# Third batch's combining weights finished among the experts, conversions paused while the first sums are copied, last store split: a fused linear-attention, soft-MoE and feed-forward kernel

## The chip, the core and the metric

The kernel runs on one core of a Trainium2 chip. The metric is device time in microseconds (us) of one execution, taken as the median of several runs. Five engines work side by side, each on its own queue in program order: TensorE (PE, matrix products, with its weight loads shown as PEld), VectorE (DVE), ScalarE (ACT), GpSimd (POOL) and SyncE (SP), which here issues all DMAs. They meet at semaphores: an instruction that has to wait holds everything behind it on its engine. PE writes to PSUM, which has eight banks of 128 x 512 floats; DVE and ACT read them out.

## The reference, cut to what matters

Three stages follow each other. `attn` is a gated linear recurrence over 768 steps for 4 batches of 8 heads of 48; its output is laid out as 3072 tokens of 384. `moe` is a soft mixture of 8 experts with 4 slots each, and `moe2` a feed-forward layer with 2048 hidden units.

```python
for t in range(S):                                   # attn
    cur = einsum('bhd,bhe->bhde', u * kt, vt)
    y[:, :, t] = einsum('bhd,bhde->bhe', rt, state + cur)
    state = wt[:, :, :, None] * state + einsum('bhd,bhe->bhde', kt, vt)
...
logits = x @ phi                                     # moe: x is 3072 x 384, phi 384 x 32
d = softmax of logits over the tokens                # dispatch: each slot's mix of tokens
slot_input = d.T @ x
slot_out[e] = relu(slot_input[e] @ w1[e]) @ w2[e]    # 8 experts
c = softmax of logits over the 32 slots              # combining weights of each token
x = c @ slot_out
...
h = x @ w_in                                         # moe2
out = (h * sigmoid(1.702 * h)) @ w_out
```

All is float32. w_in and w_out come as 8-byte floats and are turned into float32 on the chip.

## The kernel before

`phase_a` computes the recurrence in chunks and, per batch of 768 tokens, the logits. `phase_b` runs the experts on the 32 slot inputs. `phase_c` is the dense stage. There c @ slot_out is never formed as 384 columns: slot_out @ w_in is a table of 32 x 2048 (`mst`, two halves of 1024 columns), and each token needs only its 32 combining weights. The transposed combining weights of all tokens lie in `cT`; a matrix product with 128 columns of `mst` gives the hidden values of 512 tokens. To keep float32 accuracy, the operands are split into a high part (fp32r, a rounded copy) and a low part (the rest), and the terms are added by more products or, for `cT` and `mst`, by four 32-row blocks in one product.

**Combining weights of a batch** (`Batch.combining`, a generator in two parts, then `combined`): the first part subtracts each token's maximum and takes exponentials (L890 to L892). The second (L895 to L906) sums, divides, and writes high and low parts to two `c4` tiles: eight DVE instructions and two POOL copies. `combined` (L914) transposes three 128 x 128 blocks of a `c4` tile into a PSUM bank on PE, and ACT copies the bank to its home in `cT`. Batches 0 and 1 are done in `phase_a`. For batches 2 and 3 (`comb`), `phase_b` runs the first part.

**The dense stage's units.** The main loop of `phase_c` has 96 units n, each a pair (block tb of 512 tokens, block f of 128 hidden values). For units 0 to 15 the blocks f = 0 to 7 of token blocks 0 and 1 alternate; units 16 to 47 take token blocks 2 to 5 one after the other, f = 0 to 7; units 48 to 95 are f = 8 to 15 of all six. A unit is: `act` (one product into a `pa` bank, L1089; two such banks), `gelu` (ACT, L1096), `high` (ACT cast to `gh`, L1103), `low` (DVE subtraction to `gl`, L1111), and `project` (nine products of 128 x 512 into three `po` banks, L1127: `gh` with w_out's high part, `gh` with its low part, `gl` with the high part). Up to unit 15 the order is by term, later by bank. Each of `g`, `gh`, `gl` has three buffers. In unit n the order of issue is high(n+1), act(n+3), gelu(n+2), low(n+1), the specials of that unit, project(n).

After its first eight f, a token block's sums are copied from the three `po` banks to memory (`keep`, L1141: two copies on DVE, one on ACT), in units 14, 15, 23, 31, 39 and 47. After the last eight, `store` adds bank and kept sum on DVE (L1147) and stores the 128 x 512 result (L1148); three such stores per token block.

**Conversions.** In nearly every unit of the first half some step of an 8-byte-to-4-byte conversion follows project: three DVE instructions (L290, L291, L293), one on ACT (L298), two on DVE (L302, L303), and for w_out a split into high and low (ACT L194, DVE L196). Which starts when stands in `begin`; one step of each running conversion is issued per unit (`going`). Pieces of w_in's second half (`late`, three steps) start in units 12, 14, ..., 26.

**Batches 2 and 3 in the loop.** The second part of `combining` was issued in unit 17 for batch 2 and unit 25 for batch 3, and the six transposes (into `po` banks of the token block that is not in work) with two ACT copies in units 20 and 28, before project.

**The dense stage's preparation** (from the first `scaled` to the loop): folding the expert outputs, the table's first half, `keep_warm` (dummy products into a bank that nobody reads, so that PE works while it waits, L280), four `act`, two `gelu`/`high`/`low`, `project(0)`, `gelu(2)`. Its PSUM banks: `pt` and `prs[0]`, `prs[1]` for the table, and two `pa` banks, the first of which (`pm`) held the table.

Of the kernel before, what the change touches and what calls it, by code (L numbers as in the profile page):

```python
# [14 lines left out]
ALU = mybir.AluOpType  # L15
# [256 lines left out]
def run(steps):  # L272
    for _ in steps:
        pass


def keep_warm(nc, room, idle, n):

    for _ in range(n):
        nc.tensor.matmul(room, idle[:, 512:640], idle[:, 0:512], start=True, stop=True)  # L280
# [647 lines left out]
def phase_b(tc, W, after, late, sp, sT, soft, batches=(), ebias=None):  # L928
    nc = tc.nc
    con, ident, phis, cT, SI, negm, Zs = soft  # L930
    psA = after.enter_context(tc.tile_pool(name="psA", reuse_waits="tile", bufs=2, space=PSUM))
    mid = ExitStack()
    psH = mid.enter_context(tc.tile_pool(name="psH", bufs=1, space=PSUM, reuse_waits="tile"))
    psS = mid.enter_context(tc.tile_pool(name="psS", bufs=2, space=PSUM, reuse_waits="tile"))
    with late:
        bp = late.enter_context(tc.tile_pool(name="bp", bufs=1, reuse_waits="tile"))
        own = ExitStack()
        w2q = own.enter_context(tc.tile_pool(name="w2q", bufs=1, side="right", reuse_waits="tile"))
        W.load2(4 if batches else 3, pool=w2q)
        sTm = bp.tile([128, KT, NE * 36], F32, name="sTm")  # L940
        nc.gpsimd.memset(sTm, 0.0)
        hTm = bp.tile([128, HT, NE * 36], F32, name="hTm")
        h = W.slot(W.place_out[3])
        flat = hTm.rearrange("p f s -> p (f s)")
        step = W.in_steps(ebias, {0: flat, 1: flat[:, 1024:], 4: h[:, 512:]}) if batches else lambda *a: None

        def own_slots(t):

            return t.rearrange("p k (e q) -> p k e q", q=36)[:, :, :, 0:SPE]

        fold = con[:, OFF_SEL:OFF_SEL + NS]
        nc.vector.tensor_copy(own_slots(sTm), sT.rearrange("p k (e s) -> p k e s", s=SPE))

        pz = psS.tile([128, 512], F32, name="ps")
        nc.tensor.matmul(pz[:, 0:1], con[:, OFF_SEL:OFF_SEL + 128], Zs[:, B - 1:B], start=True, stop=True)
        scale = Zs[:, 0:1]
        nc.vector.tensor_scalar_add(scale, pz[:, 0:1], 1e-9)
        nc.vector.reciprocal(scale, scale)


        def room():
            return sp.tile([128, 12 * NS], F32, name="c4", bufs=3)

        comb = [bt.combining(room) for bt in batches[2:]]
        for it in comb:
            next(it)
        nc.scalar.activation(bp.tile([128, 1], F32, name="tiny"), con[:, 0:1], AF.Gelu_apprx_sigmoid)
        step(0, 0)
        step(0, 1)
        step(1, 0)  # L970
        step(1, 1)
        step(0, 2)
        ph = psH.tile([128, 512], F32, name="ps")
        for n, p in enumerate((3, 0, 1, 2)):
            for kt in range(KT):
                for j in range(4):
                    e = p + 4 * (j % 2)
                    nc.tensor.matmul(ph[32 * j:32 * j + 32], sTm[:, kt, 36 * e - 4 * p:36 * e - 4 * p + 32],  # L978
                                     W.a[e][j // 2][:, kt], start=(n == 0 and kt == 0), stop=(n == 3 and kt == KT - 1))
            if n == 0:  # L980
                step(1, 2)
                step(2, 0)
                step(2, 1)
                nc.scalar.copy(hTm, con[:, OFF_MASK:OFF_MASK + 1].unsqueeze(2).to_broadcast([128, HT, NE * 36]))
            if n == 1:
                step(2, 2)
                step(3, 0)
                if batches:
                    cT.room(1, F32R)
            W.turn(n)  # L990
        for q in range(2):
            nc.scalar.activation(h[:, 256 * q:256 * q + 256], ph[:, 256 * q:256 * q + 256], AF.Relu)
        step(3, 1)
        h4 = h[:, 0:512].rearrange("p (q c r) -> p q r c", q=2, r=2)
        for q in range(2):
            pt = psS.tile([128, 2, 128], F32, name="ps")
            for r in range(2):
                nc.tensor.transpose(pt[:, r], h4[:, q, r], ident)
            for r in range(2):
                nc.vector.tensor_copy(own_slots(hTm)[:, 2 * q + r::4].rearrange("p f (g e) s -> p f g e s", g=2),  # L1000
                                      pt[:, r].rearrange("p (f g e s) -> p f g e s", f=2, g=2, s=SPE)[:, :, :, 0:4])
        po = psH.tile([128, 512], F32, name="ps")
        for e in range(NE):
            for i0 in range(0, HT, 4):
                for j in range(4):
                    nc.tensor.matmul(po[32 * j:32 * j + 32, 0:DM], hTm[:, i0 + j, 32 * e:32 * e + 32],  # L1006
                                     W.b[e][:, i0 + j], start=(e == 0 and i0 == 0), stop=(e == NE - 1 and i0 > 0))
            if e == 0:
                rep = W.slot(W.place_c[0], F32R)
                nc.gpsimd.memset(rep[:, 0:1024].bitcast(F32), 0.0)  # L1010
                rep4 = rep[:, 0:1024].rearrange("p (q n a s) -> p q n a s", q=2, n=4, a=4)
                for i in range(2):
                    nc.gpsimd.tensor_copy(rep4[:, i, :, i::2],
                                          ident.rearrange("p (n s) -> p n s", n=4).unsqueeze(2).to_broadcast([128, 4, 2, NS]))
            for m, i in (((3, 2), (4, 0), (4, 1)), ((5, 0), (5, 1), (4, 2)), ((5, 2),))[e] if e < 3 else ():
                step(m, i)
            if e == 4:
                own.close()
                cvp = after.enter_context(tc.tile_pool(name="cvp", bufs=1, side="right", reuse_waits="tile"))
    return comb, cvp, room, psA, mid, psH, psS, po, rep  # L1020


def phase_c(tc, W, after, dense, ebias, soft, out, check=None, batches=()):
# [3 lines left out]
    with ExitStack() as c2:  # L1027
# [115 lines left out]
        def store(tb):  # L1143

            for i in range(KT):
                os_ = gp.tile([128, 512], F32, name="os", bufs=3)
                nc.vector.tensor_tensor(out=os_, in0=live["po", tb][i], in1=sums[tb][:, i], op=ALU.add)  # L1147
                nc.sync.dma_start(out=out[i * 128:(i + 1) * 128, tb * 512:tb * 512 + 512], in_=os_)  # L1148

        def open_psO():  # L1150
            nonlocal psO
# [4 lines left out]
        def bank(a, i):  # L1156
            return psO.tile([128, 512], F32, name=f"po{a}{i}")
# [23 lines left out]
        step(1, 0)  # L1181
        act(0)
        act(1)
        keep_warm(nc, pt, idle, 7)
        gelu(0)
        place(0, 1, prs[1], nc.vector.tensor_copy)
        high(0)
# [11 lines left out]
        act(3)  # L1199
        project(0)  # L1200
        gelu(2)
        step(2, 2)
        step(3, 0)

# [11 lines left out]
        for n in range(1, n_all):  # L1216
            high(n + 1)
            act(n + 3)
            gelu(n + 2)
            low(n + 1)  # L1220
            if n == t1 + 1:
                pm = bank(0, 0)
                table(1, pm)
            if n == t1 + 2:
                table_high(1, pm)
                table_low(1, pm)
            if n == t1 + 3:
                prs = [bank(0, 1 + q) for q in range(2)]
                for q in range(2):
                    repeat(1, q, prs[q])  # L1230
            if check and n == n_all - FH + 2:
                check.result(room(), bank(0, 0))
            for k, (bt, it) in enumerate(zip(batches[2:], comb)):
                if n == FH * (k + 2) + 1:
                    run(it)
                if n == FH * (k + 2) + 4:
                    for i in range(2):
                        nc.scalar.copy(bt.home(i), bt.combined(i, bank(1 - k, i)))
            project(n)
            if n == t1 + 3:  # L1240
                place(1, 0, prs[0], nc.scalar.copy)
                place(1, 1, prs[1], nc.vector.tensor_copy)
            if order[n][1] == FH - 1:
                keep(order[n][0])
            if order[n][1] == FT - 1:
                store(order[n][0])
            if n in begin:
                f, m, k = begin[n]
                going.append([f, m, 0, k])
            for q in going:  # L1250
                q[0](q[1], q[2])
                q[2] += 1
            going = [q for q in going if q[2] < q[3]]
            if check and c0 <= n < c0 + NCK:
                check.load(n - c0, room())
            if check and c0 + 2 <= n < c0 + NCK + 2:
                check.part(n - c0 - 2)
# [51 lines left out]
```

## Time and profile before

| | |
|---|---|
| runs | 430.81 us median of 3 (430.78 to 433.74) |
| the profiled execution | 430.79 us; span of its instructions 429.0 us |
| busy, share of the span | PE 399.3 us (93%), DVE 323.5 (75%), ACT 261.3 (61%), POOL 48.4 (11%) |
| mean granted TensorE clock | 0.986 of full speed |
| dense stage | from about 186 us to the end |

"Busy" of an engine counts the time in which an instruction is in it; on PE the products overlap, so what counts there is the distance from one start to the next. A row of the timeline gives start, duration, engine, line, operation, tiles, size and count; in square brackets stands how long the engine had stood idle before, and what released it. The granted clock is the share of full speed (2.4 GHz) that PE was given; 0.50 is its lower level, 1.2 GHz.

### The profile page before, as it was taken

The numbers are of one execution on the slowest core, as the hardware profiler recorded it, in microseconds if no ns is written. First come the engines' busy times: TensorE is split into PE (matmuls) and PEld (weight loads), VectorE is DVE, ScalarE is ACT, GpSimd is POOL, SyncE is SP. The second block draws the span as 40 slices with busy tenths as digits, with TensorE's granted clock in tenths as the row PEclk, the third lists the DMA queues.
The fourth block names the chain that finished last, engine by engine and source line by source line (L and its number), as shares of the span: only waits on it lengthen the run. The fifth ranks groups of instructions, "written<-read, shape, count | busy, mean of one in ns | idle before, by whom it ended". The sixth has DMA issues, their size and how long they took to land.

```text
span 429.0 us, 8870 instructions
## 1 busy us (share of the span) xinstructions
PE 399.3 (93%) x3402; PEld 305.5 (71%) x3405; DVE 323.5 (75%) x534; ACT 261.3 (61%) x620; POOL 48.4 (11%) x81
## 2 busy tenths in 40 slices
PE   5799989999889989998999999999999999999993
PEld 1566767777667764766887787787888888888872
DVE  7899999999899768959966988777765655743521
ACT  5578677887778656438765666566574544544530
POOL 4423232232222120200000000000000000000000
PEclk9699999999999999999999999999999999999997
DMA  8979879799996979999000001000001543501102
GB/s 218 212 192 252 224 202 236 224 282 277 237 306 205 355 266 402 412 410 422 38 0 0 2 1 37 2 0 20 0 0 53 162 136 93 165 14 61 73 4 82
DMA packets 24565, 67.35 MB, mean 157 GB/s; under 512 B 2848, under 2 KB 6560, under 8 KB 24256
## 3 DMA queue, kind: packets, MB, share of 16 engines
q1 hardware_dynamic: 24512, 66.67, 49.8%
q8 instruction: 29, 0.48, 0.4%
q14 instruction: 24, 0.20, 0.1%
HBM read 61.94 MB, written 4.72 MB: 155 GB/s over the span
## 4 chain that ended last, share of the span: by engine, by line
PE 70%; DMA 11%; DVE 8%; ACT 4%; issue 2%; SPq 1%; POOL 1%; DVEq 0%; ACTq 0%; POOLq 0%
PE po L1127 43%; DMA v<-in_vin 9%; PE pa L1089 5%; PE py L584 3%; PE py L579 3%; PE ps L1006 3%; PE ps L978 2%; DMA wt<-in_rkz 2%; PE pkv L549 2%; PE pg L562 2%; ACT am L534 2%; SPq L473 1%; PE ps L600 1%; DVE gl L1111 1%; PE ps L280 1%
## 5 line engine op out<-in xcount | busy, mean ns | idle before, releaser
L1111 DVE TENSOR_TENSOR gl<-g,gh 128x512 fp32r<-128x512 f32 x96 | 65.4, 688 | 40.5 <-ACT gh L1103 40.2
L1103 ACT CAST gh<-g 128x512 fp32r<-128x512 f32 x96 | 59.4, 619 | 58.9 <-PE po L1127 58.5
L1127 PE MATMUL po<-gh,wi 128*128 128x512 f32 x288 | 88.9, 390 | 0.0
L1127 PE MATMUL po<-gh,wt 128*128 128x512 f32 x288 | 84.0, 391 | 0.0
L534 ACT ACTIVATE am<-con,cT 128x128 f32<-128x128 f32 x192 | 59.4, 392 | 8.2 <-DVE cT L527 8.2
L1127 PEld LDWEIGHTS po<-gh,wi 128*128 128x128 f32 x288 | 54.2, 188 | 11.6
L1127 PEld LDWEIGHTS po<-gh,wt 128*128 128x128 f32 x288 | 54.0, 188 | 11.6 <-issue 0.4
L1096 ACT ACTIVATE g<-pa 128x512 f32<-128x512 f32 x96 | 57.1, 595 | 2.5 <-PE pa L1089 2.5
L1127 PE MATMUL po<-gl,wi 128*128 128x512 f32 x144 | 56.4, 391 | 0.0
L1127 PE MATMUL po<-gl,wt 128*128 128x512 f32 x144 | 51.6, 395 | 1.8 <-DVE gl L1111 1.7
L1089 PE MATMUL pa<-cT,wt 128*128 128x512 f32 x96 | 38.4, 402 | 1.1 <-ACT g L1096 1.1
L568 DVE COPY_PREDICATED am<-con,pg 128x768 f32<-128x768 uint32 x32 | 32.1, 1002 | 3.7 <-ACT am L534 3.7
L1127 PEld LDWEIGHTS po<-gl,wt 128*128 128x128 f32 x144 | 27.0, 188 | 9.2 <-DVE gl L1111 3.5
L1127 PEld LDWEIGHTS po<-gl,wi 128*128 128x128 f32 x144 | 27.0, 188 | 5.7
L492 POOL TENSOR_TENSOR rkb<-wt 128x384 f32<-128x384 f32 x25 | 27.9, 1118 | 13.6 <-DMA wt<-in_rkz 11.3
L501 DVE TENSOR_TENSOR_SCAN wt<-wt 128x774 f32<-128x774 f32 x16 | 28.4, 1772 | 0.5
L498 DVE TENSOR_TENSOR_SCAN wt<-wt 128x774 f32<-128x774 f32 (+1 forms) x17 | 28.1, 1655 | 0.2 <-DMA wt<-in_z 0.2
L579 PE MATMUL py<-am,v 128*64 128x128 f32 x384 | 27.8, 278 | 0.0
L562 PE MATMUL pg<-wt 64*128 64x128 f32 x312 | 25.1, 295 | 0.5 <-DVE am L568 0.5
L601 ACT COPY xb<-ps 128x288 f32<-128x288 f32 x28 | 11.2, 399 | 22.8 <-PE ps L600 22.8
L562 PEld LDWEIGHTS pg<-wt 64*128 64x128 f32 x312 | 20.0, 192 | 5.4 <-issue 2.8
L1147 DVE TENSOR_TENSOR os<-po,wt 128x512 f32<-128x512 f32 x18 | 12.4, 692 | 13.7 <-PE po L1127 13.7
(206 smaller groups left out, 579.1 us busy)
## 6 DMA issues: line engine op xcount, KB each, us to landing
wt<-in_w SPq DMA_DIRECT2D x21, 512.0 KB, 7.3
wt<-in_w SPq DMA_DIRECT2D x13, 768.0 KB, 8.7
wt<-in_rkz SPq DMA_DIRECT2D x26, 288.0 KB, 5.2
v<-in_vin SPq DMA_DIRECT2D x16, 296.0 KB, 5.5
c<-in_wc SPq DMA_DIRECT2D x24, 192.0 KB, 2.5
out_dram<-os SPq DMA_DIRECT2D x18, 256.0 KB, 2.1
wt<-in_rkz SPq DMA_DIRECT2D x30, 145.3 KB, 3.7
wi<-in_w_in SPq DMA_DIRECT2D x6, 512.0 KB, 6.6
```

Of the source, the lines that this page charges most:

```text
L492: eng.tensor_tensor(out=rkb[:, c], in0=st[p]["r"][:, c], in1=st[p]["k"][:, c], op=ALU.mult)
L498: nc.vector.tensor_tensor_scan(out=sf[:, o:n][:, ::-1], data0=z[:, o + 1:n + 1][:, ::-1], data1=dS[:, o:n][:, ::-1], initial=0.0, op0=ALU. ...
L501: nc.vector.tensor_tensor_scan(out=x, data0=z[:, 0:XL], data1=dX, initial=0.0, op0=ALU.mult, op1=ALU.add)
L534: nc.scalar.activation(am[:, j, c], ident, AF.Copy, scale=q["coef"][:, c0 + c, j:j + 1])
L562: nc.tensor.matmul(q["pg"][:, j, (c - c0) * CH:(c - c0 + 1) * CH], q["k"][64 * j:64 * j + 64, c * CH:(c + 1) * CH], q["r"][64 * j:64 * j + ...
L568: nc.vector.copy_predicated(q["am", c0], later, q["pg"][:, :, 0:3 * CH].rearrange("p j (c t) -> p j c t", t=CH))
L579: nc.tensor.matmul(py[64 * j:64 * j + 64, (c - c0) * CH:(c - c0 + 1) * CH], q["v"][:, c * 96 + j * 48:c * 96 + j * 48 + 64], q["am", c0][: ...
L1089: nc.tensor.matmul(pa, mst[:, f * 128:(f + 1) * 128], cT.at(tb * 512, 512), start=True, stop=True)
L1096: nc.scalar.activation(g, live[n], AF.Gelu_apprx_sigmoid)
L1103: nc.scalar.copy(gh, live[n])
L1111: nc.vector.tensor_tensor(out=gl, in0=g, in1=gh.bitcast(F32), op=ALU.subtract)
L1127: nc.tensor.matmul(live["po", tb][i], w[:, i * 128:(i + 1) * 128], g, start=(f % FH == 0 and k == 0), stop=(f % FH == FH - 1 and k == 2))
```

## The change

Four edits, all in the way work is ordered. (1) The second part of batch 2's combining runs in `phase_b`, after the products of expert 3, in place of unit 17. (2) Its six transposes are issued in the preparation right behind `act(1)`, into the banks `pt` and `prs[0]`, and ACT copies them out right behind `gelu(2)`; of the seven `keep_warm` products that stood there, three are left, and they write to the table's bank `pm`. Batch 3 stays in units 25 and 28. (3) In units 14, 15 and 16 no conversion step is issued; what was running or would start goes on in unit 17. (4) The very last store is made in two halves of 256 columns.

```diff
@@ -1014,6 +1014,9 @@
             for m, i in (((3, 2), (4, 0), (4, 1)), ((5, 0), (5, 1), (4, 2)), ((5, 2),))[e] if e < 3 else ():
                 step(m, i)
+            if e == 3:
+                for it in comb[0:1]:
+                    run(it)
             if e == 4:
                 own.close()
@@ -1144,8 +1147,11 @@
             for i in range(KT):
                 os_ = gp.tile([128, 512], F32, name="os", bufs=3)
-                nc.vector.tensor_tensor(out=os_, in0=live["po", tb][i], in1=sums[tb][:, i], op=ALU.add)
-                nc.sync.dma_start(out=out[i * 128:(i + 1) * 128, tb * 512:tb * 512 + 512], in_=os_)
+                m = 2 if tb == n_tb - 1 and i == KT - 1 else 1
+                for t in range(0, 512, 512 // m):
+                    c = slice(t, t + 512 // m)
+                    nc.vector.tensor_tensor(out=os_[:, c], in0=live["po", tb][i][:, c], in1=sums[tb][:, i, c], op=ALU.add)
+                    nc.sync.dma_start(out=out[i * 128:(i + 1) * 128, tb * 512 + t:tb * 512 + t + 512 // m], in_=os_[:, c])
@@ -1181,7 +1187,9 @@
         act(0)
         act(1)
-        keep_warm(nc, pt, idle, 7)
+        for bt in batches[2:3]:
+            live["pct"] = [(bt.home(i), bt.combined(i, t)) for i, t in enumerate((pt, prs[0]))]
+        keep_warm(nc, pm, idle, 3 if batches else 7)
         gelu(0)
@@ -1199,6 +1207,8 @@
         act(3)
         project(0)
         gelu(2)
+        for home, pct in live.pop("pct", ()):
+            nc.scalar.copy(home, pct)
         step(2, 2)
@@ -1230,12 +1240,12 @@
-            for k, (bt, it) in enumerate(zip(batches[2:], comb)):
-                if n == FH * (k + 2) + 1:
+            for bt, it in zip(batches[3:], comb[1:]):
+                if n == FH * 3 + 1:
                     run(it)
-                if n == FH * (k + 2) + 4:
+                if n == FH * 3 + 4:
                     for i in range(2):
-                        nc.scalar.copy(bt.home(i), bt.combined(i, bank(1 - k, i)))
+                        nc.scalar.copy(bt.home(i), bt.combined(i, bank(0, i)))
@@ -1247,7 +1257,7 @@
-            for q in going:
+            for q in going if n not in (FT - 2, FT - 1, FT) else ():
```

Three places show how the instructions move. In brackets stands on whose semaphore an instruction waits; "Activation" is ACT, the numbers behind tile names tell buffers apart. First PE in the preparation, from `act(0)` and `act(1)` to the start of `project(0)`. Before (the rows of the last six `keep_warm` are left out):

```order
L1089 MATMUL pa<-cT_2250,wt_2540 128x512 [waits Activation_49]
L1089 MATMUL pa<-cT_2250,wt_2540 128x512 [waits PE_49]
L280 LDWEIGHTS con
L280 MATMUL ps<-con 128x512
...
L1089 MATMUL pa<-cT_2250,wt_2540 128x512 [waits Activation_49] x2
L1127 MATMUL po_2656<-gh,wt_2542 128x512
L1127 MATMUL po_2657<-gh,wt_2542 128x512 [waits PE_49]
L1127 MATMUL po_2658<-gh,wt_2542 128x512 [waits PE_49]
L1127 MATMUL po_2656<-gh,wt_2543 128x512 [waits DVE_49]
```

And with the change (two more `keep_warm` left out):

```order
L1092 MATMUL pa<-cT_2250,wt_2553 128x512 [waits Activation_49] x2
L914 MATMUL ps<-con,c_2503 128x128 [waits Pool_49]
L914 MATMUL ps<-con,c_2503 128x128 x2
L914 MATMUL ps<-con,c_2507 128x128 [waits Pool_49]
L914 MATMUL ps<-con,c_2507 128x128 x2
L280 LDWEIGHTS con
L280 MATMUL pa<-con 128x512
...
L1092 MATMUL pa<-cT_2250,wt_2553 128x512 [waits Activation_49]
L1092 MATMUL pa<-cT_2250,wt_2553 128x512 [waits PE_49]
L1130 MATMUL po_2671<-gh,wt_2555 128x512
L1130 MATMUL po_2672<-gh,wt_2555 128x512 [waits Activation_49]
```

`act(1)` now waits for ACT: since `pm` is written again by `keep_warm`, its bank is not free, and `act(0)`, `act(1)` and `act(2)` all take the other `pa` bank. `project(0)`'s second product takes the bank of `prs[0]` (bank 3) and now waits for ACT, before for PE. The semaphore value it waits for is that of the second copy of the next piece.

The second place is ACT behind `gelu(1)` and its cast. Before:

```order
L194 CAST wt_2542<-cv_f 128x384
L298 ACTIVATE cv_e<-cv_e,ebias 128x384
L1096 ACTIVATE g<-pa 128x512
L1103 CAST gh<-g 128x512
L1096 ACTIVATE g<-pa 128x512
```

With the change:

```order
L194 CAST wt_2555<-cv_f 128x384
L298 ACTIVATE cv_e<-cv_e,ebias 128x384
L1099 ACTIVATE g<-pa 128x512
L1211 CAST cT_2401<-ps 128x384 x2
L1106 CAST gh<-g 128x512
L1099 ACTIVATE g<-pa 128x512
```

The two copies of batch 2's weights stand between `gelu(2)` and `high(2)`, behind a conversion step (L298) of DVE's making. The third place is DVE from `keep(0)` (unit 14) to unit 17. Before:

```order
L1141 COPY wt_83<-po_2656 128x512
L1141 COPY wt_83<-po_2658 128x512
L302 SCALAR_TENSOR_TENSOR cv_e<-wt_82,cv_e 128x384
L303 TENSOR_TENSOR wt_82<-cv_f,cv_e 128x384
L290 TENSOR_SCALAR cv_e<-wt_82 128x384
L291 TENSOR_SCALAR cv_f<-wt_82 128x384
L293 SCALAR_TENSOR_TENSOR cv_f<-wt_82,cv_f 128x384
L1111 TENSOR_TENSOR gl<-g,gh 128x512
L1141 COPY wt_83<-po_2685 128x512
L1141 COPY wt_83<-po_2687 128x512
L1111 TENSOR_TENSOR gl<-g,gh 128x512
```

With the change:

```order
L1144 COPY wt_83<-po_2671 128x512
L1144 COPY wt_83<-po_2673 128x512
L1114 TENSOR_TENSOR gl<-g,gh 128x512
L1144 COPY wt_83<-po_2702 128x512
L1144 COPY wt_83<-po_2704 128x512
L1114 TENSOR_TENSOR gl<-g,gh 128x512 x2
L302 SCALAR_TENSOR_TENSOR cv_e<-wt_82,cv_e 128x384
L303 TENSOR_TENSOR wt_82<-cv_f,cv_e 128x384
L290 TENSOR_SCALAR cv_e<-wt_82 128x384
L291 TENSOR_SCALAR cv_f<-wt_82 128x384
L293 SCALAR_TENSOR_TENSOR cv_f<-wt_82,cv_f 128x384
```

Five conversion instructions between the copies of `keep(0)` and the next `gl` have gone behind `low(18)`; in unit 17 one conversion ends and two start, where before one step at most ended and one started.

## Rows read from the trace of the kernel before

**Rows 1.** The page's part 4: shares of the chain that ended last, by engine.

```profile
PE 70%; DMA 11%; DVE 8%; ACT 4%; issue 2%; SPq 1%; POOL 1%; DVEq 0%; ACTq 0%; POOLq 0%
```

**Rows 2.** The same chain in order of time, one piece: start, us, work.

```profile
218.97 2.05 PE po L1127 x9
```

**Rows 3.** Timeline of PE at the start of the dense stage's units.

```profile
194.60 0.50 PE L1089 MATMUL pa<-cT,wt 128*128 128x512 f32 x1 [0.35 <-ACT g L1096]
...
197.93 0.50 PE L1089 MATMUL pa<-cT,wt 128*128 128x512 f32 x1 [0.77 <-ACT g L1096]
198.26 1.55 PE L1127 MATMUL po<-gh,wt 128*128 128x512 f32 x6
...
200.34 0.40 PE L1089 MATMUL pa<-cT,wt 128*128 128x512 f32 x1
```

**Rows 4.** Timeline of ACT in the same stretch.

```profile
193.97 0.58 ACT L1096 ACTIVATE g<-pa 128x512 f32<-128x512 f32 x1
...
196.78 0.62 ACT L298 ACTIVATE cv_e<-cv_e,ebias 128x384 int32<-128x384 int32 x1 [0.90 <-DVE cv_e L290]
197.30 0.58 ACT L1096 ACTIVATE g<-pa 128x512 f32<-128x512 f32 x1
```

**Rows 5.** Lines L1238 and L914: ns min/median/max, first and last start.

```profile
L1238 ACT CAST cT<-po x4: 467/478/492, 244.3 to 263.9; 128x384 fp32r<-128x384 f32 x4
```

**Rows 6.** Timeline of PE, units 16 to 21.

```profile
232.26 0.40 PE L1089 MATMUL pa<-cT,wt 128*128 128x512 f32 x1
...
233.86 0.50 PE L1127 MATMUL po<-gl,wt 128*128 128x512 f32 x1 [0.75 <-DVE gl L1111]
...
241.44 0.50 PE L1127 MATMUL po<-gl,wt 128*128 128x512 f32 x1 [0.38 <-DVE gl L1111]
...
243.41 0.82 PE L914 MATMUL po<-con,c 128*128 128x128 f32 x6
...
246.12 0.40 PE L1089 MATMUL pa<-cT,wt 128*128 128x512 f32 x1
```

**Rows 7.** Timeline of DVE during the experts.

```profile
182.84 0.69 DVE L303 TENSOR_TENSOR wi<-wi 128x512 f32<-128x512 f32 x1
185.60 0.36 DVE L290 TENSOR_SCALAR cv_e<-wt 128x384 int32<-128x384 int32 x1 [2.06 <-DMA wt<-in_w_out]
```

**Rows 8.** Timeline of DVE, units 14 to 18.

```profile
229.72 1.29 DVE L1141 COPY wt<-po 128x512 f32<-128x512 f32 x2 [3.34 <-PE po L1127]
230.92 0.55 DVE L302 SCALAR_TENSOR_TENSOR cv_e<-wt,cv_e 128x384 int32<-128x384 int32 x1
...
231.99 0.35 DVE L290 TENSOR_SCALAR cv_e<-wt 128x384 int32<-128x384 int32 x1
...
233.12 0.68 DVE L1111 TENSOR_TENSOR gl<-g,gh 128x512 fp32r<-128x512 f32 x1
...
238.31 0.34 DVE L895 TENSOR_REDUCE sm<-l 128x6 f32<-128x192 f32 x1
...
240.63 0.75 DVE L1111 TENSOR_TENSOR gl<-g,gh 128x512 fp32r<-128x512 f32 x1
```

**Rows 9.** Windows: us; busy of PE, PEld, DVE, ACT, POOL; granted clock, DMA share, GB/s.

```profile
11.00:12.00 1.00, 1.00 (x9) 0.67 (x9) 1.00 (x1) 1.00 (x4) 0.00 (x0) 0.57 1.05 240
...
17.00:18.00 1.00, 1.00 (x4) 0.30 (x2) 1.00 (x1) 0.00 (x0) 0.00 (x0) 0.52 0.83 190
...
424.00:425.00 1.00, 0.00 (x0) 0.00 (x0) 0.00 (x0) 0.00 (x0) 0.00 (x0) 0.58 0.10 33
```

**Rows 10.** Timeline of PE around one of its longest waits.

```profile
152.65 0.55 PE L600 MATMUL ps<-con,xt 128*128 128x128 f32 x3 [1.81 <-ACT xt L587]
```

**Rows 11.** Timeline, the last addition before the last store.

```profile
421.65 0.69 DVE L1147 TENSOR_TENSOR os<-po,wt 128x512 f32<-128x512 f32 x1 [0.67 <-PE po L1127]
```

**Rows 12.** Line L1148: the stores' issue (ns) and time to landing (us), min/median/max.

```profile
L1148 SPq DMA_DIRECT2D out_dram<-os x18: 332/339/968, 330.2 to 422.4; - x18
...
DMA to landing us min/median/max: 2.0/2.1/2.9
```

## The prediction, made before the result was known

> **What bounds the kernel.** I read the chain of waits first. PE makes up 70% of it [rows 1], and in the dense stage it runs in pieces of nine products in 2.05 us [rows 2]: 0.228 us from start to start, 2.28 for the ten products of a unit. Where PE stands in such a row, only what lets it wait, or gives it other products, is worth anything; work moved on DVE or ACT alone is worth nothing. So I went through PE's timeline for waits. There are two places that this change touches. In the preparation, PE waits 0.77 us before 197.93, for `gelu(2)` on ACT [rows 3]; that gelu ended at 197.30 + 0.58 = 197.88 and was itself late, since the conversion step ahead of it had waited 0.90 us for DVE [rows 4]. From 198.26 on PE is the bound. In units 16 to 21 PE waits again, for `gl` at 233.86 and 241.44, and has six transposes at 243.41 [rows 6]; there DVE is the late one, with copies of `keep`, conversions and the combining in front of `low` [rows 8].
>
> **The change, part by part.** The sum is made against the profiled execution, 430.79 us; the median of the runs is 430.81, so the two can be taken as one.
>
> *Units 16 to 21.* From `act` of unit 16 at 232.26 to that of unit 21 at 246.12 are 13.86 us [rows 6]; five units without waits are 5 x 2.28 = 11.40. The excess is 2.46: the wait at 233.86, caused by two conversion halves between `keep(0)` and `low` (230.92 to 233.12), the wait at 241.44, caused by the 2.3 us of combining (238.31 to 240.63) [rows 8], and the transposes, 0.6 us. All three causes leave this stretch. Late next would be `low` in units 17 to 20, into which the held conversions go: four second halves of 1.07 us (230.92 to 231.99) and four first ones of 1.13 (231.99 to 233.12), with four `low` of 0.6, are 11.2 us against 9.1 of PE. `gl` and `gh` have three buffers, so DVE may be two units, 4.6 us, ahead, and with only `keep` and `low` to do in units 14 to 16 it gets there. Worked through unit by unit, `low` is done 0.6 us or more before PE wants it. Term: **-2.5**, bounds -2.5 and -1.5 (one of the waits comes back).
>
> *The combining among the experts.* DVE stands idle 2.06 us until 185.60, for a DMA [rows 7]; the eight instructions need 2.3. The conversion behind them is 0.3 late and ends near 187.1, still ahead of the next thing that DVE does for PE. The two POOL copies find POOL empty. Term: 0.
>
> *The preparation.* This is where the change adds a wait. `act(1)` now takes the bank of `act(0)` and waits for `gelu(0)`; `act(2)` takes it again and waits for `gelu(1)`, which started at 193.97 [rows 4] and released the product at 194.60 [rows 3]. So far nothing is lost: `act(3)` waited for that same gelu before. Six transposes in place of four `keep_warm` lie in these waits and cost nothing. Then `project(0)` starts its first product near 195.1, and the second needs the bank that ACT must empty first. On ACT the two copies come behind `gelu(2)`, and that cannot move ahead: it stands behind the conversion step at 196.78 that waits for DVE [rows 4]. So the copies start near 197.30 + 0.48 = 197.78 (on ACT, starts follow each other some 0.1 before an end, as 196.78 and 197.30 show). Each takes 0.48 [rows 5], the second is done at 198.64, and PE goes on at 198.69. Eight products remain, the first after a wait with 0.33 to the next (197.93 to 198.26 [rows 3]), seven with 0.228: `act(4)` at 200.62. It was at 197.93, but there PE paid the 0.10 of restarting too. Everything queued on PE behind it, all later units, comes 2.69 - 0.10 = 2.6 us later, and as PE is the bound from there, nothing gives it back. ACT itself gets 0.9 us of copies more there and loses them in unit 20, at no cost. Term: **+2.6**, bounds +2.3 and +2.9 (copies overlapped or one after the other).
>
> *The clock.* PE now stands still from 195.3 to 198.7, 3.4 us, longer than any wait in the dense stage before. The granted clock fell to its lower level at the end of the program, some 2.5 us after the last product (0.58 in the window from 424 [rows 9], the last product a little before 421.65 [rows 11]), and near 11 us after a stretch of scattered work; it did not fall in a wait of 1.81 us [rows 10]. 3.4 us is nearer to the first. Once low, it stayed low from 11 to 18 us [rows 9], 6.8 us, with PE waiting in part of that time; here PE has work without a break, so I take half, 3.4 us. At half speed half the products get done in that time: **+1.7**, an estimate, bounds 0 (it doesn't fall) and +3.4 (low for 6.8 us).
>
> *The last store.* The last addition takes 0.69 [rows 11], two halves some 0.06 more, and a second issue on SP (0.34 [rows 12]) starts about 0.1 later than the whole one did; behind it is only the end of the program. A store landed 2.0 to 2.9 us after its issue [rows 12]; the last one is the 2.9, as data still flows in the window from 424 [rows 9]. Bounds: +0.1 (2.9 again) and -0.8 (2.0). I take **-0.3**, nearer to the row of the same place. The Trainium skill, page "DMA: Bandwidth & Descriptors", section "Anatomy of one DMA — SWDGE (gpsimd) path", speaks against cutting up a small transfer: about 2.0 us are fixed and only the bytes, at 436 GB/s, shrink. By that fit (for another issuing engine) half of 256 KB saves 0.3 less the 0.1, an estimate, and the sum would be 0.1 higher; the 2.1 us median of rows 12 agrees with a cost that is mostly fixed.
>
> Sum: 430.79 - 2.5 + 0 + 2.6 + 1.7 - 0.3 = **432.3 us**.
>
> **The rivals.**
>
> A. *The wait is there, the clock stays up.* For it: a wait of 1.81 us left it alone [rows 10]. Against: at the end it had fallen some 2.5 us after the last product [rows 9, 11]. 430.79 - 2.5 + 2.6 - 0.3 = 430.6. The Trainium skill, page "TensorE: Matmul & The Clock Gate", section "HAM oscillation — how this bites in real kernels", has a PE that waits for data between bursts start each burst at the lower rate; by it A would go and the forecast stand. No run here shows such a wait inside the dense stage.
>
> B. *Slower: the clock stays low long.* At `project(0)`, right after the wait, PE at half speed with ACT and DVE still catching up may look idle enough to be held down, as it was from 11 to 18 us [rows 9]. Low for 6.8 us it costs 3.4: 430.79 - 2.5 + 2.6 + 3.4 - 0.3 = 434.0. From 8.8 us of low clock on, it is more than 1% slower (+4.3). Against: PE has products without a break there.
>
> C. *The conversions do not rest but pile up.* The change only shifts three units' steps into unit 17, and if DVE is less far ahead than I worked out, a wait of about 1 us is back in units 19 to 22: 433.2. For it: DVE was busy nearly all the time in that stretch [rows 8]. Against: the 0.6 us margin, and that PE comes later while DVE doesn't.
>
> D. *The new wait is not paid.* If the copies were done before PE wanted the bank, only the gains would stand: 430.79 - 2.5 - 0.3 = 428.0. Against: `gelu(2)` ended at 197.88 in the trace, and the product that used to start near 195.2 waits for something behind it.
>
> **How the numbers follow.** Forecast 0.50, A 0.25, B 0.11, C 0.08, D 0.06. The likeliest gives 432.3. The range: D (0.06) falls out below, and of B and the forecast's upper tail some 0.1 above; A with the tail's bounds reaches down to 430.1, B's centre is 434.0. So 430.0 to 434.0. A measurement of this kernel can tell about 1% (4.3 us) from no change: faster than 426.5 needs more than D, 0.02; slower than 435.1 needs B beyond 8.8 us, or B and C together, 0.05; within 1%, 0.93.
>
> **What would show it.** Right, if the changed profile has PE idle some 3.4 us in the middle of `project(0)` with ACT's cT copies (L1211) as the releaser, a granted clock near 0.5 in a stretch of some 3 us after 198 us, and units 16 to 21 in 11.4 us with no wait on `gl`; the last store would land some 0.3 us sooner after the last product. Wrong in the preparation, if `project(0)` runs through or ACT copies before 197; wrong in the loop, if waits on `gl` stand in units 17 to 22; wrong in the clock, if it stays at 1.00 (then A).

## The result, and the profile after

The changed kernel took 434.6 us (median of 20 runs, 431.2 to 436.2). The kernel before, run beside it 20 times, took 431.65 (429.9 to 434.1). The ratio is 1.0059, 95% interval [1.0037, 1.0080], which is 1.6 to 3.5 us slower. The ratios here and below leave out one slow run of the kernel before, of 1271.55 us, beside e5 to e8. The profiled execution took 435.39, with a span of 433.4. The forecast was 432.3, or 1.0035 of the execution that it was summed against; the median lies 0.6 us above the end of its range.

The places of [rows 3, 6] have a counterpart each. PE's timeline in the preparation of the changed kernel (start, duration, line, operation, tiles, in brackets idle time and releaser):

```profile
194.37 0.50 PE L1092 MATMUL pa<-cT,wt 128*128 128x512 f32 x1
195.56 0.50 PE L1092 MATMUL pa<-cT,wt 128*128 128x512 f32 x1 [0.69 <-ACT g L1099]
195.90 0.82 PE L914 MATMUL ps<-con,c 128*128 128x128 f32 x6
...
197.21 0.73 PE L1092 MATMUL pa<-cT,wt 128*128 128x512 f32 x2
197.78 0.39 PE L1130 MATMUL po<-gh,wt 128*128 128x512 f32 x1
201.29 2.30 PE L1130 MATMUL po<-gh,wt 128*128 128x512 f32 x5 [3.12 <-ACT cT L1211]
203.39 1.48 PE L1130 MATMUL po<-gl,wt 128*128 128x512 f32 x3
204.67 0.53 PE L1092 MATMUL pa<-cT,wt 128*128 128x512 f32 x1
```

And ACT there, to be held against [rows 4]:

```profile
199.39 0.62 ACT L298 ACTIVATE cv_e<-cv_e,ebias 128x384 int32<-128x384 int32 x1 [0.90 <-DVE cv_e L290]
199.91 0.58 ACT L1099 ACTIVATE g<-pa 128x512 f32<-128x512 f32 x1
200.39 0.85 ACT L1211 CAST cT<-ps 128x384 fp32r<-128x384 f32 x2
```

`project(0)` starts one product and then stands for 3.12 us until ACT has emptied the bank; ACT's copies come behind a `gelu` that waits behind a conversion step. The five products after the wait take 2.30 us, where six took 1.55 in [rows 3]: the clock. Windows of the same execution (us; busy time and count of PE, PEld, DVE, ACT, POOL; granted clock; DMA share; GB/s), to be held against [rows 9]:

```profile
11.00:20.00 9.00, 6.69 (x45) 4.28 (x47) 7.95 (x8) 5.00 (x16) 3.21 (x3) 0.50 0.85 200
153.80:157.10 3.30, 3.23 (x25) 1.97 (x27) 3.06 (x11) 0.71 (x3) 0.91 (x2) 0.50 0.88 318
157.20:201.50 44.30, 38.79 (x454) 25.11 (x455) 36.16 (x89) 22.13 (x46) 4.88 (x8) 1.00 0.95 377
201.60:204.90 3.30, 3.30 (x9) 2.53 (x8) 1.37 (x3) 2.19 (x5) 0.00 (x0) 0.50 0.97 403
205.00:210.00 5.00, 5.00 (x23) 4.08 (x22) 4.20 (x9) 3.42 (x7) 0.00 (x0) 1.00 0.48 192
```

The fourth line is the fall that the forecast had put there; the clock fell at 201.54, 0.25 us after PE had gone on at 201.29, and stayed low for 3.41 us. The first two lie in the recurrence, long before anything that was changed. In [rows 9] the low clock ended near 18 us; here it reaches beyond 20, and at 153.8 it falls once more. So everything is already late when the dense stage begins: `act(0)` stands at 194.37, before at 191.77.

In the loop the waits of [rows 6] are gone. Here is PE in the stretch that [rows 6] showed (the same five units, from `act` in unit 16 to `act` in unit 21), and then DVE at `keep(0)` and the `low` behind it:

```profile
239.04 0.40 PE L1092 MATMUL pa<-cT,wt 128*128 128x512 f32 x1
...
239.73 0.39 PE L1130 MATMUL po<-gl,wt 128*128 128x512 f32 x1
...
246.57 0.39 PE L1130 MATMUL po<-gl,wt 128*128 128x512 f32 x1
...
250.44 0.40 PE L1092 MATMUL pa<-cT,wt 128*128 128x512 f32 x1
```

```profile
236.50 1.29 DVE L1144 COPY wt<-po 128x512 f32<-128x512 f32 x2 [3.34 <-PE po L1130]
237.87 0.69 DVE L1114 TENSOR_TENSOR gl<-g,gh 128x512 fp32r<-128x512 f32 x1
```

11.40 us, five units of 2.28. `low` follows `keep` at once, with no conversion between them, as there was in [rows 8].

At the end stand four stores where there were three; the last additions and the row of the stores, to be held against [rows 11, 12]:

```profile
426.01 0.76 DVE L1153 TENSOR_TENSOR os<-po,wt 128x256 f32<-128x256 f32 x2 [0.67 <-PE po L1130]
```

```profile
L1154 SPq DMA_DIRECT2D out_dram<-os x19: 332/337/387, 334.5 to 426.9; - x19
...
DMA to landing us min/median/max: 2.0/2.1/2.8
```

The longest landing is 2.8 us, before 2.9. So hardly anything came sooner, and there is an issue more.

**The program by stages.** Since the start of the dense stage moves from one execution to the next, I measured from `act(0)` on. act(k) is the k-th product of that line; it is issued in unit k - 3, so act(16) to act(24) spans the loop's specials. "End" is the span less the start of the last product (421.23 before, 425.58 with the change). All in us, from one profile each; the names are those of the experiments below.

| | act(0) at | act(0) to act(16) | act(16) to (24) | act(30) to (47) | end | act(0) to end of span |
|---|---|---|---|---|---|---|
| before | 191.77 | 33.65 | 20.70 | 43.40 | 7.79 | 237.25 |
| before, again (e4) | 193.49 | 33.64 | 20.72 | 43.43 | 7.66 | 237.12 |
| rest only (e3) | 192.96 | 33.65 | 20.86 | 43.41 | 7.60 | 237.26 |
| combining only (e12) | 194.44 | 33.65 | 20.05 | 43.39 | 7.87 | 236.63 |
| store only (e9) | 191.56 | 33.64 | 20.72 | 43.41 | 8.11 | 237.55 |
| the change | 194.37 | 37.83 | 18.24 | 43.39 | 7.85 | 239.06 |
| the change, again (e5) | 194.12 | 37.84 | 18.24 | 43.40 | 8.41 | 239.56 |
| without rest (e6) | 192.10 | 37.82 | 19.37 | 43.45 | 7.83 | 240.14 |
| with one store (e10) | 193.70 | 37.83 | 18.24 | 43.41 | 7.62 | 238.85 |
| wait filled (e2) | 190.93 | 36.19 | 18.25 | 43.40 | 7.93 | 237.45 |
| copies early (e1) | 192.98 | 34.19 | 18.24 | 43.36 | 8.02 | 235.53 |
| gelu first (e7) | 191.07 | 32.90 | 18.24 | 43.41 | 9.29 | 235.59 |
| rest more (e8) | 193.60 | 32.91 | 18.24 | 42.49 | 7.62 | 232.97 |
| all waits (e11) | 194.96 | 32.91 | 18.23 | 43.00 | 7.89 | 233.74 |

The three columns in the middle repeat within 0.1 us, most within 0.02, wherever the kernels agree in that stage. The first doesn't repeat at all. The end repeats within 0.3 us where there is one last store, and not within a microsecond where there are two halves.

The first column goes with the clock. Where it was low for 6.8 us in all before the dense stage (four profiles), `act(0)` stands at 190.9 to 191.8; for 10.2 us (three), at 192.1 to 193.0; for 13.7 us (seven), at 193.5 to 195.0. Kernels with the preparation of before and with that of the change are in each group.

### The profile page after: what moved, and what is told of

Its sections match the earlier page's. It is cut to its first block, busy times and chain, and to the rows that moved or that the text cites. A ratio compares the mean times of both kernels' runs of the same rounds, so it can differ in the third digit from the quotient of the medians.

```text
span 433.4 us, 8867 instructions
## 1 busy us (share of the span) xinstructions
PE 402.0 (93%) x3398; PEld 308.2 (71%) x3401; DVE 324.2 (75%) x535; ACT 261.7 (60%) x620; POOL 48.1 (11%) x81
## 4 chain that ended last, share of the span: by engine, by line
## 5 line engine op out<-in xcount | busy, mean ns | idle before, releaser
L1130 PE MATMUL po<-gh,wt 128*128 128x512 f32 x288 | 85.0, 394 | 3.1 <-ACT cT L1211 3.1
L492 POOL TENSOR_TENSOR rkb<-wt 128x384 f32<-128x384 f32 x25 | 27.6, 1105 | 15.9 <-DMA wt<-in_rkz 13.7
L579 PEld LDWEIGHTS py<-am,v 128*64 128x64 f32 x384 | 21.2, 139 | 2.6 <-issue 0.6
```

Of the source, the lines that this page charges most:

```text
L492: eng.tensor_tensor(out=rkb[:, c], in0=st[p]["r"][:, c], in1=st[p]["k"][:, c], op=ALU.mult)
L579: nc.tensor.matmul(py[64 * j:64 * j + 64, (c - c0) * CH:(c - c0 + 1) * CH], q["v"][:, c * 96 + j * 48:c * 96 + j * 48 + 64], q["am", c0][: ...
L1130: nc.tensor.matmul(live["po", tb][i], w[:, i * 128:(i + 1) * 128], g, start=(f % FH == 0 and k == 0), stop=(f % FH == FH - 1 and k == 2))
```

## The experiments

Ratios are to the kernel before, timed beside each, with their 95% intervals.

**e1, copies early.**

```diff
         gelu(1)
+        for home, pct in live.pop("pct", ()):
+            nc.scalar.copy(home, pct)
         step(1, 2)
...
         gelu(2)
-        for home, pct in live.pop("pct", ()):
-            nc.scalar.copy(home, pct)
```

> The changed kernel with one thing moved: ACT's two copies of the transposed weights stand right behind gelu(1), ahead of its cast, instead of behind gelu(2). Theory (the terms of the forecast): the copies then end about 0.1 us after project(0)'s first product, PE waits in the preparation only for gelu(2) as before the change (0.8 us), the granted clock stays at 1.00 there, act(4) comes 6.2 us after act(0) (10.3 in the changed kernel), and what is left is the gain of the loop: 0.994 of before (-2.5 us). Rival (something else in the change costs a further 1 us, whatever the preparation does): the wait goes all the same, but the time is 0.997 of before (-1.4 us). Rival (the wait was hidden and the clock fell for another reason): the clock still falls for 3.4 us near 200 us, and the time is about 1.001.

Measured: 430.84 us, 0.9986 [0.9960, 1.0012]. The wait on the copies and the fall of the clock are gone; act(0) to act(16) went from 37.83 to 34.19. act(4) came after 6.71 us, not 6.2: the copies now push `high(1)` back, and the conversion step ahead of `gelu(2)`, which waits 1.09 us for DVE, starts 5.55 us after `act(0)`, not 5.02 as with the change. A window with the clock at 1.00, and that step on ACT:

```profile
19.30:425.00 405.70, 386.90 (x3339) 300.03 (x3337) 309.12 (x519) 250.43 (x596) 40.14 (x68) 1.00 0.49 156
```

```profile
198.53 0.61 ACT L298 ACTIVATE cv_e<-cv_e,ebias 128x384 int32<-128x384 int32 x1 [1.09 <-DVE cv_e L290]
```

The dense stage is 1.7 us shorter than before. The ratio says 0.6, and its interval just reaches 1.7; the 2.5 that was expected lies outside it, and by it alone the first rival (1.4 us) stands as well.

**e2, the wait filled.**

```diff
         act(3)
+        keep_warm(nc, prs[1], idle, 12)
         project(0)
```

> The changed kernel with 12 more dummy products (some 2.6 us) between act(3) and project(0): ACT's copies stay where they are, so PE still cannot go on before the second copy ends, but it stands idle for 0.5 us only. Theory (wait and clock are two costs, 2.6 and 1.7 us, and the clock falls because PE stands idle): act(4) comes 8.6 us after act(0), the granted clock stays at 1.00 around 205 us, and the time is 1.000 of before (+2.6 of wait, -2.5 of loop). Rival (the clock falls for another reason than PE's idle time): it falls for 3.4 us all the same, 1.004. Rival (a further 1 us elsewhere): no fall of the clock there, 1.0025.

Measured: 432.1 us, 1.0015 [0.9993, 1.0036]. PE, and windows of that execution:

```profile
194.32 2.76 PE L280 MATMUL ps<-con 128*128 128x512 bf16 x12
196.73 0.58 PE L1130 MATMUL po<-gh,wt 128*128 128x512 f32 x1
197.83 1.41 PE L1130 MATMUL po<-gh,wt 128*128 128x512 f32 x5 [0.52 <-ACT cT L1212]
```

```profile
191.00:197.00 6.00, 5.31 (x27) 2.87 (x26) 4.98 (x11) 4.42 (x9) 0.00 (x0) 1.00 1.05 432
197.00:200.00 3.00, 2.48 (x11) 1.80 (x10) 2.48 (x6) 3.00 (x8) 0.00 (x0) 1.00 0.95 404
200.00:205.00 5.00, 5.00 (x23) 4.14 (x22) 4.29 (x9) 3.70 (x8) 0.00 (x0) 1.00 0.79 323
```

The copies end as late as ever, but PE works in the meantime, the clock stays at 1.00, and the five products take 1.41 us in place of 2.30. So the two costs come apart: 37.83 - 36.19 = 1.64 us is the clock, 36.19 - 33.65 = 2.54 the wait. The ratio is too wide to tell the theory (1.000) from the rival of a further 1 us (1.0025).

**e3, the rest of the conversions alone** (in the kernel before).

```diff
-            for q in going:
+            for q in going if n not in (FT - 2, FT - 1, FT) else ():
```

> The kernel before with only the rest of the conversions in units 14 to 16; combining in unit 17, transposes in unit 20 and one last store as before. Theory (the conversions made the wait of unit 16, 0.75 us and its restart, and DVE gets far enough ahead to hide the combining too): units 16 to 21 take 12.0 us, 11.4 and the six transposes; 0.9956 of before (-1.9 us). Rival (the combining alone makes the second wait): 12.5 us, 0.997 (-1.3). Rival (the held conversions and the combining pile up in units 17 to 20): 13.3 us or more, 0.9985 to 1.000. In all three the preparation is that of before: act(4) 6.2 us after act(0), no fall of the clock near 200 us.

Measured: 431.4 us, 0.9988 [0.9961, 1.0015]; 20.86 us from act(16) to act(24), nothing gained. The last rival was right. DVE does `keep` and `low` early, but the combining (236.32 to 238.64) and the held conversions then stand in one row, and PE waits in unit 19:

```profile
242.78 0.50 PE L1127 MATMUL po<-gl,wt 128*128 128x512 f32 x1 [1.64 <-DVE gl L1111]
```

**e4, the kernel before again**, with no edit.

> The kernel before, unchanged, as a measure of what one execution differs from the next. Theory (the changed kernel's profiled execution was 2.6 us late at act(0) by chance, through the clock's low stretches in the recurrence): the ratio is 1.000 within 0.2%, and in this profile act(0) may lie anywhere from 191.8 to 194.4 us, as the clock was low for 6.8 or 10.2 us near 10 us and fell or did not fall near 154 us. Rival (the change itself makes the recurrence slower): act(0) stands near 191.8 us again, and in all kernels with the change near 194.4 us.

Measured: 432.4 us, 1.0007 [0.9977, 1.0037]; act(0) at 193.49, where the first profile of the same program had 191.77. The unchanged program showed what the profile of the change had shown in the recurrence, so the change isn't needed for it (windows as above):

```profile
11.00:21.00 10.00, 7.90 (x54) 5.28 (x56) 8.27 (x8) 4.98 (x16) 3.47 (x4) 0.50 0.90 208
154.30:157.60 3.30, 3.30 (x30) 2.27 (x26) 3.02 (x12) 0.48 (x1) 1.23 (x3) 0.50 0.64 232
```

**e5, the change again**, with no edit.

> The changed kernel, unchanged, a second time. The dense stage, from act(0) to the last instruction, took 237.3 and 237.1 us in two executions of the kernel before and 239.1 in the one of the change (+1.9). Theory (what the change does lies in the dense stage, the rest of its first ratio is chance in the recurrence): the ratio is 1.0044 (+1.9 us) or a little less, since the clock need not fall in every execution; the dense stage is 239.1 us with a fall of the clock, 237.4 without. Rival (the change costs a further 0.7 us or more outside the dense stage): 1.006 or above again.

Measured: 434.1 us, 1.0064 [1.0028, 1.0100]. The preparation and the loop repeat to 0.01 us, and the clock falls again for 3.4 us at `project(0)`. The end took 8.41 us; SP's issue of the very last store, the second half, lasted 1.0 us in place of 0.4. The ratio itself lies where the rival had it (1.006 or above), but the theory's 1.0044 is inside its interval, and the medians, 434.1 beside 432.3, differ by 1.8 us only. So a cost outside the dense stage is neither shown nor excluded.

**e6, the change without the rest.** (The condition of e3 taken out again.)

> The changed kernel without the rest of the conversions in units 14 to 16; the combining stays among the experts and the transposes in the preparation. Theory (each edit takes one wait: the rest that of unit 16, the moved combining that of unit 19): the wait on gl in unit 16, 1.06 us with its restart, is back, and act(16) to act(24) take 19.3 us (20.7 before, 18.2 with the change): 1.0068 of before. Rival (PE comes 4.1 us later to the loop and DVE does not, so DVE is ahead and the rest is not needed): 18.2 us and 1.0044. Rival (the moved combining alone does nothing): 20.0 us or more, 1.0085.

Measured: 435.4 us, 1.0072 [1.0045, 1.0099]; 19.37 us, as the theory had it. The wait of unit 16 is back, at the size of [rows 6]:

```profile
238.36 0.50 PE L1130 MATMUL po<-gl,wt 128*128 128x512 f32 x1 [0.75 <-DVE gl L1114]
```

**e7, gelu first** (beside the edit of e1).

```diff
-        step(2, 1)
         act(3)
         project(0)
         gelu(2)
+        step(2, 1)
```

> The kernel with the copies behind gelu(1), and in addition gelu(2) ahead of the conversion step on ACT (L298) that waits there for DVE. Theory (act(4) waits for gelu(2) alone, and gelu(2) for that step): act(4) comes 5.5 us after act(0), in place of 6.7 with the copies behind gelu(1) alone and 6.2 before the change; dense stage 234.4 us, 0.9935 of before (-2.8 us). Rival (the delayed conversion step makes DVE late for low(2) or low(3)): act(4) to act(8) grow from 9.24 to 9.8 us or more, 0.996.

Measured: 428.9 us, 0.9925 [0.9896, 0.9954]. `project(0)` runs through and `act(4)` follows without a wait:

```profile
194.47 1.61 PE L1130 MATMUL po<-gh,wt 128*128 128x512 f32 x6
195.91 0.85 PE L1130 MATMUL po<-gl,wt 128*128 128x512 f32 x3
196.60 0.40 PE L1092 MATMUL pa<-cT,wt 128*128 128x512 f32 x1
```

5.53 us after `act(0)`, as expected; the dense stage is longer than expected (235.6 for 234.4) by its end alone, 9.29 us, in which the second half's issue took 1.9 us (ns, the longest of 19):

```profile
L1154 SPq DMA_DIRECT2D out_dram<-os x19: 332/338/1905, 326.3 to 418.7; - x19
```

**e8, rest more.** The kernel of e7 with `m = 1` in `store` and

```diff
-            for q in going if n not in (FT - 2, FT - 1, FT) else ():
+            for q in going if n not in (FT - 2, FT - 1, FT, FH * 3 + 1, FH * 4 - 1) else ():
```

> As the kernel with gelu(2) first, with one last store in place of two halves, and with the conversions resting also in unit 25 (where the fourth batch's weights are finished) and unit 31 (first sums kept). Theory (the two waits on gl in that stretch, 0.4 and 0.9 us with restart, are of the same kind as those that the change took away; a second half store only adds an issue): act(30) to act(47) take 42.1 us in place of 43.4, the time from the last product to the end 7.6 to 7.8 us in place of 7.85 to 8.0, dense stage 232.8 us, 0.990 of before (-4.4 us). Rival (the steps held back make new waits two or three units later): 43 us or more, 0.9925. Rival (two halves do land sooner): 8.0 us or more from the last product to the end.

Measured: 427.8 us (six runs), 0.9886 [0.9841, 0.9931], faster than both kernels. The rest in unit 31 took the 0.9 us away (a wait of 0.61 us and its restart, in unit 33); the one in unit 25 did nothing, as by the order of issue the step that stands ahead of the combining is that of unit 24. 42.49 us, not 42.1.

**e9, the halved store alone**, in the kernel before; and **e10, the change with one store** (`m = 1`).

> The kernel before with only its last store in two halves. From the last product to the last instruction, kernels with one last store took 7.6 to 7.8 us (four profiles), those with two halves 7.85 to 9.3 (six). Theory (the second half is a further issue and further closing waits on SP, and in some executions SP's second issue itself takes 1 to 2 us in place of 0.4): 7.85 us or more here too; the dense stage 237.3 to 238.8 us; time 1.000 to 1.003 of before. Rival (the longer end has to do with the other edits): 7.6 to 7.8 us.

> The changed kernel with one last store, as before. Theory: 7.6 to 7.8 us from the last product to the last instruction; dense stage 238.9 us where the clock falls in the preparation, 237.2 where it does not; time 1.004 to 1.005 of before. Rival (the end is longer through the other edits): 7.85 us or more.

Measured: e9 432.2 us, 1.0011 [0.9982, 1.0040], end 8.11 us; e10 433.7 us, 1.0041 [1.0016, 1.0066], end 7.62. Both ends are as the theory had it; the ratios are too wide to show so little.

**e11, all waits.** e8 with `FH * 3` in place of `FH * 3 + 1` and without `keep_warm(nc, pm, idle, 3)`.

> As the kernel with the conversions resting in more units, but resting in unit 24 in place of 25 (the step issued there stood ahead of the fourth batch's combining), and without the three dummy products into the table's bank, so that act(1) does not wait for gelu(0). Theory: act(0) to act(4) take 5.2 us (5.5 with the dummies), act(30) to act(47) 42.1 (42.5), the dense stage 232.3 us; 0.989 of before (-4.9 us). Rival (without the dummy products PE stands idle more and the clock falls in the preparation): granted clock 0.5 near 200 us, 234 us, 0.993. Rival (the step held back in unit 24 makes a wait later): 42.5 us or more.

Measured: 428.6 us, 0.9925 [0.9902, 0.9949]. A miss. act(4) came after 5.54 us as in e8: `act(3)` is earlier, but the copies aren't, and `project(0)` waits for them. Resting in unit 24 gave a wait back later:

```profile
261.25 0.50 PE L1130 MATMUL po<-gl,wt 128*128 128x512 f32 x1 [0.62 <-DVE gl L1114]
```

The clock stayed at 1.00 from 160 us to the last products, without the dummies too. By its dense stage (232.97 us to 233.74) e8 remains the best; the intervals of the two ratios overlap.

**e12, the combining alone** (in the kernel before).

```diff
+            if e == 3:
+                for it in comb[0:1]:
+                    run(it)
...
-                if n == FH * (k + 2) + 1:
+                if n == FH * (k + 2) + 1 and k:
```

> The kernel before with only the second part of the third batch's combining moved among the experts; its transposes stay in unit 20, no rest of the conversions, one last store. Theory (each of the two edits of the loop is worth something only beside the other: the rest alone gave 20.9 us from act(16) to act(24), the combining and the transposes moved without the rest 19.4, all together 18.2): the transposes are 0.65 us of products, the wait of unit 16 stays, so 20.0 us (20.7 before), the preparation 6.2 us, the stretch from the last product of the recurrence to the folding of the expert outputs 30.2 us as in every kernel so far; 0.998 of before (-0.7 us). Rival (the combining in unit 17 did not make the second wait): 20.7 us and 1.000. Rival (the combining among the experts costs time there): 30.5 us or more to the folding.

Measured: 431.6 us, 0.9988 [0.9964, 1.0013]; 20.05 us, as expected.

## Why the prediction was wrong

Right was the mechanism in the preparation and in the loop, and three terms of the sum:

- *The loop*, -2.5: measured 18.24 - 20.70 = -2.46. It takes both edits. The moved combining alone is worth 0.65 (e12), the transposes out of the loop 0.68 more (20.05 in e12, 19.37 in e6), and the rest 1.13 on top of both (e6 against the change), but alone nothing (e3). Rival C, conversions that pile up, is what e3 shows; it doesn't happen once the combining is away.
- *The combining among the experts*, 0: DVE ran it from 186.06, and the copy that serves PE still stood waiting for PE behind it:

```profile
186.06 0.35 DVE L895 TENSOR_REDUCE sm<-l 128x6 f32<-128x192 f32 x1
...
188.38 0.42 DVE L290 TENSOR_SCALAR cv_e<-wt 128x384 int32<-128x384 int32 x1
...
190.24 0.26 DVE L1063 COPY c<-ps 128x96 f32<-128x96 f32 x1 [0.57 <-PE ps L1061]
```

  From the start of the last product of the recurrence (L584) to that of the folding of the expert outputs are 30.2 us in all fourteen profiles, with and without it.
- *The wait*, +2.6: measured +2.54 (e2 against before). *The clock*, +1.7: measured +1.64 (e2). The clock fell in all four profiles that have the wait of 3.12 us, each time for 3.41 us, and in none where it was filled or taken away. So rivals A and D fell, and B too: no profile has 6.8 us there. B's number, 434.0, came nearest to the measured one all the same, by chance. One of the four, e10, as a window:

```profile
201.80:205.00 3.20, 3.20 (x9) 2.46 (x8) 1.91 (x4) 1.79 (x4) 0.00 (x0) 0.50 0.98 402
```

  The Trainium skill, page "TensorE: Matmul & The Clock Gate", section "HAM oscillation — how this bites in real kernels", has bursts after a wait start at the lower rate; the trace agrees nearly, with 2.30 us for five products that took 1.41 in e2, but the first 0.25 us of the burst (0.7 to 1.1 in the other three profiles) still ran at 1.00.

  Two things in this term were luck. That the clock stays low for half of the 6.8 us was a choice, for which the forecast had no row. And the row that was held against a fall, the wait of 1.81 us that "left it alone" [rows 10], speaks for neither side: all fourteen profiles have that wait, and in seven of them the clock was low for 3.4 us from about its end on (falling between 0.2 us before and 1.3 us after PE went on), in e4, with the unchanged program, among them. After it the way to the last product of L584 took 5.2 to 5.3 us in place of 3.8.

Two steps failed, the baseline and the term of the last store. Each is larger than the 0.6 us by which the median lies above the range: the baseline was 0.86 us too low, the store's term 0.8.

- *The last store*, forecast -0.3 with bounds +0.1 to -0.8: the seven profiles with one last store have an end of 7.60 to 7.89 us, mean 7.72, the seven with two halves 7.83 to 9.29, mean 8.21. That is **+0.5** (+0.4 by the medians; the two profiles of the result alone, 7.85 and 7.79, would show 0.06), on the other side, outside the bounds. The step that failed is that half a store lands sooner: the second half landed 3.0 us after its issue in the mean of the seven profiles, the whole store 2.95. Of the +0.5, 0.2 lie ahead of the last landing and 0.3 behind it, which I had taken as unchanged. There SP passes semaphores one after the other, some 0.07 us each; in the profile of the change seven of them are passed from the end of the last long wait on, in that of before three, and four times 0.07 is 0.3. In two of the seven profiles the second issue itself took 1.0 and 1.9 us in place of 0.4. That halving causes this isn't shown, since an earlier, whole store took 0.8 to 1.1 us to issue in five profiles (0.97 in [rows 12]). The Trainium skill, page "DMA: Bandwidth & Descriptors", section "Anatomy of one DMA — SWDGE (gpsimd) path", has most of such a transfer's cost fixed, for another issuing engine; the trace agrees at least that halving it saved nothing.
- *"The median of the runs is 430.81, so the two can be taken as one."* Of the three runs shown one was 433.74. Over 20 runs the median is 431.65, and 431.7 to 432.3 beside the later experiments. The execution that I summed against was a quick one: its `act(0)` stood at 191.77, and in other executions at 190.9 to 195.0, while act(0) to act(16), where the edits leave it alone, repeats to 0.01. The range held the doubts about the change, not those about the baseline.

In rival B a small sum is off as well: 1% slower takes 9.0 us of low clock by its own terms, not 8.8.

Put right, the sum is -2.46 + 2.54 + 1.64 + 0.5 = **+2.2 us**, against 1.6 to 3.5 by the ratio (+2.5 at its centre), and on 431.65 it gives 433.9. The 0.7 us to 434.6 I can't assign. They are inside the ratio's interval. If they are more than chance, they may lie ahead of the experts, where the clock moves `act(0)` about: the five profiles with the preparation of before have it at 191.6 to 194.4, the nine others at 190.9 to 195.0, and these overlap too much to tell.

## What to carry to other kernels

Ask of each moved copy what stands ahead of it on its engine, not how long it takes: 0.9 us of copies cost 4.2 here, since they stood behind a step that waited for DVE; 3.6 of it went when they were moved ahead of that step (e1), and all of it when `gelu(2)` was put ahead of the step too (e7). A wait that leaves PE idle can be paid twice, once as time and once in clock: always at 3.12 us in these profiles, in seven of fourteen at 1.81, never in the dense stage's other waits, up to 1.64 (e3). Dummy products gave the second part back. Measure a stage from its own first instruction, since what lies ahead of it can move the whole time by more than the edit does.

## What was not expected of the hardware

The unchanged program started its dense stage at 191.77 us in one execution and at 193.49 in the next, and over all fourteen profiles the start lies anywhere within 4 us. It goes with the granted clock of TensorE in the recurrence: low for 6.8 us or for 10.2 near 10 us, and in half of the profiles low for 3.4 us more near 154 us, behind a wait that all of them have. And the issue of a store on SP, 0.33 to 0.39 us as a rule, took 0.8 to 1.1 us once in six profiles and 1.9 us in a seventh.
